# Squares of three blocks folded to 64 columns, rows of two blocks scaled on another engine, and an addition moved by a tile, in the first layer of a two-layer transformer kernel

## The chip, the cores and the metric

The kernel runs on one core of a Trainium2 chip. The metric is the device time of one execution in microseconds (us); the time given for a kernel is the median of its runs. A profile is one execution taken by the hardware profiler, with its own time. Engines are named as the profile names them: PE (TensorE, the matrix engine), PEld (its weight loads), DVE (VectorE), ACT (ScalarE), POOL (GpSimd) and SP (SyncE, which only issues transfers). Each takes its instructions in the order of the program and waits at an instruction whose inputs are not ready.

## The reference

Input x has 2048 tokens of 448 features. Two layers, with the same weights, each do

```python
x = x + A(layernorm(x), wqkv, wo)
x = x + B(layernorm(x), w_gate, w_up, w_down)

def A(x, wqkv, wo):
    q, k, v = heads(x @ wqkv)
    p = softmax(q @ k.T * 28 ** -0.5)
    return heads_back(p @ v) @ wo

def B(x, w_gate, w_up, w_down):
    return (sigmoid(x @ w_gate) * (x @ w_up)) @ w_down
```

with 16 heads of 28 features in A and 1792 hidden features in B.

## The kernel before, in words

**Blocks and tiles.** The 2048 tokens are four blocks of 512 (`TB` = 4 tiles of 128 tokens each). This text counts blocks and tiles from one; in the code block 1 is `b` = 0 and tile 1 is `i` = 0. The stages follow each other: projection of the first layer (about 12 to 120 us of the span), attention over 16 heads, output projection, the gated part, and the same for the second layer. The change lies in the projection of the first layer, function `project`.

**Queries and keys.** For each block `qk` (its loop begins at L865) makes 7 tiles of 128 features by 512 tokens. A tile is 11 matmuls (`by_features`, L649) into one of four PSUM banks in turn. ACT copies it to f16 (L883), DVE writes the rest that f16 loses (L884), ACT squares the copy (L886), and DVE folds the square by taking the larger of two halves (L890): once, from 512 to 256 columns. SP stores both f16 parts (L893). Three tiles later PE sums the folded squares of each head (`norm_products`, L845 and L848): one matmul of 256 columns for a tile, two for the fourth. At the end of a block DVE takes the largest of these sums (`finish`, L904). They bound the scores: `guard_of_norms`, in the first tile of the values of block 3, ends the sums of block 4, and the attention begins behind it.

**Values.** `vals` makes four tiles of 128 tokens by 448 features for each block (L671 to L676), which ACT copies out (L1136).

**Preparing a block.** Blocks 3 and 4 are normalised along the way. `norm` makes mean and variance of each of four row tiles on DVE (L340, L341) and the reciprocal deviation on POOL (L344, L346). `squares` scales each row tile on DVE (`scale`, L381) and turns it in squares of 32 on DVE (L398); `store` writes the result to DRAM and `gather` reads it back with features on the partitions, both on SP; `ready` splits it in f16 parts, ACT (L234, L239) and DVE (L235, L240) in turn. `norm_two` and `lift` (L366), used by the second layer, scale on ACT instead, with an offset that POOL works out (L355, L357).

**Measure** reads weight rows and adds up their squares on DVE (`add`, L1318 and L1322), six additions of 1.3 to 2.2 us.

**Order.** All orders are written out by hand. `along_values` and the lists `fill` tell what is issued behind which tile. Block 3: `norm` behind the third tile of the values of block 1, `squares` and `store` behind the fourth, `gather` behind the first tile of `qk` of block 2, `ready` behind its tiles 6 and 7. Block 4: `norm` behind tile 2 of `qk` of block 2, `squares` behind tiles 3 and 4, `store` behind tile 7, `gather` in the values of block 2, `ready` behind tiles 2 and 3 of `qk` of block 3. The six additions stand behind tiles 5, 6, 7 of block 3 and 1, 2, 3 of block 4.

Of the kernel before, what the change touches and what calls it, by code (L numbers as in the profile page):

```python
# [11 lines left out]
F32 = mybir.dt.float32  # L12
# [3 lines left out]
AF = mybir.ActivationFunctionType  # L16
ALU = mybir.AluOpType
AX = mybir.AxisListType

P = 128  # L20
# [7 lines left out]
TB = NT // NB  # L28
W = TB * P
# [48 lines left out]
ALONE = 3  # L78
CHUNK = D * NF // 7
SUMS_AT = ((("w", 3), 74), (("u", 0), 122), (("u", 6), 236))  # L80

N_SLOTS = 19
N_QUART = 12
# [44 lines left out]
def interleaved_layers(ctx: ExitStack, tc: tile.TileContext, x_in, wqkv, wo, w_gate, w_up,  # L128
                       w_down, out):
    nc = tc.nc  # L130
# [8 lines left out]
    uid = [0]  # L139
# [175 lines left out]
    class Block:  # L315
# [16 lines left out]
        def norm(self, js=range(TB)):  # L332
# [12 lines left out]
                                    op1=ALU.mult)  # L345
            nc.gpsimd.tensor_tensor(rs, rs, nhalf[:, c], op=ALU.pow)  # L346

        def norm_two(self, j):

            self.norm((j, j + 1))  # L350
            if j == 0:
                self.off = cpool.tile([P, TB], F32, name=f"off_{uid[0]}", tag="off", bufs=4)
                self.lifted = {}
            off = self.off[:, j:j + 2]
            nc.gpsimd.tensor_tensor(off, self.mv[:, j:j + 2, 0], self.rs[:, j:j + 2],  # L355
                                    op=ALU.mult)
            nc.gpsimd.tensor_scalar(off, off, -1.0, None, op0=ALU.mult)  # L357

        def lift(self, j):
            if self.apart:  # L360
# [30 lines left out]
        def squares(self, js=range(TB)):  # L391
            if js[0] == 0:
                self.xn = big.get("xn", [P, TB, D])
                self.xs = big.get("xs", [P, NQ, TB, 32])
            xn, xs = self.xn, self.xs
            for j in js:
                self.scale(j)
                nc.vector.transpose(xs[:, :, j, :], xn[:, j, :])  # L398
            if js[-1] < TB - 1:
                return  # L400
            big.put(xn)
# [419 lines left out]
    def project(layer, wq, begun):  # L821
# [12 lines left out]
        def qk(b, blk, fill, before, ahead=()):  # L834
            pn = [bank(4 + 2 * (b % 2), "qnorm"), bank(5 + 2 * (b % 2), "knorm")]
            late = deque()
            few = W // 2

            def rows_of_heads(i):

                return ind[:, i:i + P // H, :].rearrange("p a h -> p (a h)")

            def norm_products(i, sq):
                if i <= 3:
                    nc.tensor.matmul(pn[0][:, 0:few], rows_of_heads(i), sq[:, 0:few],  # L845
                                     start=(i == 0), stop=(i == 3))
                if i >= 3:
                    nc.tensor.matmul(pn[1][:, 0:few], rows_of_heads(1 + i), sq[:, 0:few],  # L848
                                     start=(i == 3), stop=(i == 6))
                qrt.put(sq)  # L850

            def products(pm, i, some=range(11)):
                c = slice(i * P, (i + 1) * P)
                by_features(pm, blk, lambda kt: wq.qk[0][:, kt, c],
                            lambda kt: wq.qk[1][:, kt, c], some)

            begun = deque()
            if layer == 0 and b == 0:
                begun.extend(bank(i, "qkp") for i in range(2))
                for i, some in ((0, (0, 3, 1, 6, 2, 5, 8, 4)), (1, (0, 3, 6)), (0, (7,)),  # L860
                                (1, (1, 4, 7)), (0, (9, 10))):
                    products(begun[i], i, some)
            rest = {0: (), 1: (2, 5, 8, 9, 10), 4: (0, 3, 6, 1, 4, 7, 9, 2, 5, 8, 10)}

            for i in range(7):  # L865
                c = slice(i * P, (i + 1) * P)
                pm = begun.popleft() if begun else bank(evac[0] % 4, "qkp")
                evac[0] += 1
                if layer == 0 and b == 0:
                    products(pm, i, rest.get(i, range(11)))  # L870
                else:
                    products(pm, i)
                if layer == 0 and b == 0:
                    along[i]()
                if before and i in (1, 2):
                    before(i == 2)
                if len(late) == 3:
                    late.popleft()()
                hl = qrt.get("qkhl", [P, 2, W], F16)
                sq = qrt.get("sq", [P, W], BF16)  # L880
                if i < len(ahead) and ahead[i]:
                    ahead[i]()
                nc.scalar.activation(hl[:, 0, :], pm, AF.Copy, scale=PS)  # L883
                nc.vector.scalar_tensor_tensor(hl[:, 1, :], pm, PS, hl[:, 0, :], op0=ALU.mult,  # L884
                                               op1=ALU.subtract)
                nc.scalar.activation(sq, hl[:, 0, :], AF.Square)  # L886

                for n in (W // 2, P):
                    if n >= few:
                        nc.vector.tensor_tensor(sq[:, 0:n], sq[:, 0:n], sq[:, n:2 * n],  # L890
                                                op=ALU.max)
                n = slice(b * W, (b + 1) * W)
                nc.sync.dma_start(qk_scr[c, :, n], hl)  # L893
                qrt.put(hl)
                late.append(lambda i=i, sq=sq: norm_products(i, sq))
                if i < len(fill) and fill[i]:
                    fill[i]()

            def finish(whole=True):

                while len(late) > (0 if whole else 1):
                    late.popleft()()
                for i in range(2 if whole else 0):
                    nc.vector.tensor_reduce(peaks[:, i, b:b + 1], pn[i][0:H, 0:few], axis=AX.X,  # L904
                                            op=ALU.max)
            return finish
# [260 lines left out]
        if layer == 0:  # L1167
            def scaled(*js):
                if js[0] == 0:
                    b1.xn = big.get("xn", [P, TB, D])  # L1170
                for j in js:
                    b1.scale(j)

            def turned(kts):
                b1.turn_banks(6, kts)
                for j in range(TB):
                    b1.turn(j)
                b1.turned_high()
                b1.turned_low()

            fill = [idle, idle, lambda: b1.norm([0, 1]), lambda: b1.norm([2, 3]),
                    lambda: scaled(0)]
            ahead = [idle] * 5 + [lambda: scaled(1, 2, 3)]
            tell = Measure()
            along_values = {0: lambda: (b1.parts(), turned([0, 1]), tell.read(2)),
                            1: lambda: (turned([2, 3]), big.put(b1.xn), tell.read(2)),
                            2: lambda: (fin(), b2.norm(), tell.read()),
                            3: lambda: (b2.squares(), b2.store(), tell.read())}
        if layer == 0:
            fin = qk(0, blks[0], fill, None, ahead)  # L1190
            vals(0, blks[0], along_values)
            fill = [b2.gather, b3.norm, sq(3, 0, 1), sq(3, 2, 3), idle,
                    lambda: b2.ready(0, 1), lambda: (b2.ready(2, 3), b3.store())]
            fin = qk(1, b1, fill, None)
            vals(1, b1, {0: b3.gather, 2: fin})
            add = tell.add
            fin = qk(2, b2, [idle, lambda: b3.ready(0, 1), lambda: b3.ready(2, 3), idle, add, add,
                             add], None)
            fin = qk(3, blks[3], [add, add, add], fin)
        else:  # L1200
            b2.clear()
            ones_of_values()
            b3.apart = True
            h2, h3, s3 = b2.half_steps(), b3.half_steps(), b3.squared()
            both = lambda *steps: lambda: [do() for do in steps]
            order = (3, 0, 1, 6)
            fin = qk_sums(0, blks[0], {0: b1.later + s3[0:1], 1: h2[0:1], 2: h2[1:2], 3: s3[1:2],
                                       4: h2[2:3], 5: [s3[2], s3[3], s3[6]]})
            vals(0, blks[0], {0: both(s3[4], s3[7]), 1: both(s3[5], s3[8], h2[3]),
                              2: both(fin, s3[9], b3.store, h2[4]),  # L1210
                              3: both(h2[5], b3.gather, b3.clear)}, banks=order)
            fin = qk_sums(1, b1, {0: h2[6:7], 1: h2[7:8], 3: h2[8:9], 4: h2[9:10]})
            vals(1, b1, {1: both(fin, h3[0]), 2: both(*h3[1:3]), 3: both(*h3[3:5])}, banks=order)
            fin = qk_sums(2, b2, {0: h3[5:6], 1: h3[6:7], 2: h3[7:8], 3: h3[8:9], 4: h3[9:10]},
                          None, True)
            fin = qk_sums(3, b3, {}, fin)
# [1101 lines left out]
```

## Time and profile before

| | us |
|---|---|
| median of 3 runs (1869.34 to 1869.78) | 1869.38 |
| the profiled execution, its own time | 1869.45 |
| its span, from the first to the last instruction | 1867.7 |
| PE busy in the span | 1861.4 |
| PEld busy | 1416.1 |
| DVE busy | 1462.4 |
| ACT busy | 1404.2 |
| POOL busy | 306.4 |

The table is read from the top: between the profiled execution's own time and its span lie 1.75 us of start and end, and its time stands 0.07 us above the median. PE is busy almost all the time, but the ends of its matmuls are modelled, so that its share says little by itself; what counts is how far apart its matmuls start, and who is late in each stage.

### The profile page before, as it was taken

To read this page: it belongs to the slowest core of one execution; us is meant where nothing else is said; L and a number is where in the kernel's file an instruction comes from. 1 tells how busy PE (TensorE), PEld (TensorE's weight loads), DVE (VectorE), ACT (ScalarE), POOL (GpSimd) and SP (SyncE) were. 2 spreads that over 40 slices of the span, in tenths; PEclk is the share of its full clock that TensorE was granted. 3 is DMA by queue.
4 is the path that set the end of the run, shared out by engine and by line. 5 is a ranking of instruction groups with operands and counts; after the bars stand their busy time and mean duration, and the time that the engine had idled before them with its cause. 6 is when DMAs were issued, how large, how long until landed. Compare 5 with 4: busy or idle time off the path is not lost. (4 is left out here: it accounts for less than half of the span.)

```text
span 1867.7 us, 57157 instructions
## 1 busy us (share of the span) xinstructions
PE 1861.4 (100%) x24479; PEld 1416.1 (76%) x24479; DVE 1462.4 (78%) x2933; ACT 1404.2 (75%) x1865; POOL 306.4 (16%) x582
## 2 busy tenths in 40 slices
PE   9999999999999999999999999999999999999999
PEld 4455566656565899999987568888877668999999
DVE  7748898998997888788877477777777688887764
ACT  6569999999993655555567899999999746555541
POOL 3001123453412111212122000000000031121110
PEclk9999999999999999999999999999999999999999
DMA  7674454454433866757764322122120258677653
GB/s 265 182 214 130 131 160 128 125 156 113 136 129 86 288 211 229 244 204 257 243 187 109 88 52 52 27 53 52 30 50 14 79 165 264 210 249 239 235 201 144
DMA packets 114885, 286.24 MB, mean 153 GB/s; under 512 B 15134, under 2 KB 68878, under 8 KB 114496
## 3 DMA queue, kind: packets, MB, share of 16 engines
q0 software_dynamic: 35088, 174.86, 27.8%
q1 hardware_dynamic: 78384, 106.27, 20.3%
q8 instruction: 194, 3.18, 0.7%
q10 hardware_dynamic: 1152, 1.38, 0.3%
q14 instruction: 67, 0.55, 0.1%
HBM read 218.20 MB, written 54.29 MB: 146 GB/s over the span
## 5 line engine op out<-in xcount | busy, mean ns | idle before, releaser
L1574 ACT ACTIVATE prob_s<-sc 128x1536 f32<-128x1536 f32 (+1 forms) x657 | 888.1, 1484 | 5.9 <-PE sc L1559 3.0
L1609 PE MATMUL acc<-prob_s,val_s 128*32 128x256 f32 (+3 forms) x7708 | 587.2, 384 | 0.0
L1559 PE MATMUL sc<-qp_s 114*32 114x512 f16 x7868 | 571.3, 379 | 0.0
L1559 PEld LDWEIGHTS <-qp_s 114*32 114x32 f16 x8192 | 309.9, 96 | 168.8 <-issue 70.8
L1609 PEld LDWEIGHTS acc<-prob_s,val_s 128*32 128x32 f32 x7708 | 314.1, 110 | 100.3 <-issue 9.2
L1944 PE MATMUL dnp<-dn_s,hparts_s 128*128 128x224 f16 x2184 | 245.8, 259 | 0.0
L664 PEld LDWEIGHTS <-gue_s 128*128 128x128 f16 x2240 | 218.8, 98 | 24.5 <-PE op L1738 0.7
L1944 PEld LDWEIGHTS <-hparts_s 128*128 128x128 f16 x2184 | 210.2, 98 | 5.1
L664 PEld LDWEIGHTS <-gul_s 128*128 128x128 f16 x2016 | 197.0, 98 | 19.9
L664 PE MATMUL chain<-xwide_s,gue_s 128*128 128x256 f16 x1680 | 210.9, 273 | 0.0
L1589 DVE SCALAR_TENSOR_TENSOR power_q<-power_q,expo_q 128x512 f32<-128x512 f32 x243 | 168.2, 692 | 8.3
L664 PE MATMUL side<-xshort_s,gul_s 128*128 128x256 f16 x1344 | 165.0, 273 | 0.0
L2017 ACT COPY one_q<-chain 128x256 f32<-128x256 f32 x224 | 83.1, 372 | 105.4 <-PE chain L664 104.6
L2033 DVE TENSOR_TENSOR one_q<-side,one_q 128x512 f32<-128x512 f32 x112 | 74.3, 689 | 39.1 <-PE side L664 38.8
L1638 DVE STREAM_TRANSPOSE oturned_q<-acc 128x512 f32<-128x512 f32 x32 | 23.0, 717 | 98.4 <-PE acc L1609 98.2
L2044 ACT ACTIVATE one_q<-one_q 128x512 f32<-128x512 f32 x56 | 35.3, 630 | 79.8 <-DVE one_q L2033 79.8
L1609 PE MATMUL acc<-power_q,val_s 128*32 128x256 f32 (+3 forms) x300 | 94.2, 396 | 0.0
L1584 DVE TENSOR_SCALAR expo_q<-aside,base 128x512 f32<-128x512 f32 x81 | 60.6, 748 | 40.5 <-PE aside L1559 40.1
L587 POOL TENSOR_SCALAR rs<-mv 128x1 f32<-128x1 f32 x8 | 1.5, 191 | 505.8 <-DVE mv L585 505.8
L664 PE MATMUL chain<-xshort_s,gul_s 128*128 128x256 f16 x672 | 82.5, 273 | 0.0
L1902 DVE TENSOR_TENSOR hparts_s<-hsums_q,hparts_s 128x256 f16<-128x256 f32 (+1 forms) x152 | 71.3, 519 | 11.1 <-ACT hparts_s L1898 11.1
L664 PE MATMUL side<-xwide_s,gue_s 128*128 128x256 f16 x560 | 79.4, 273 | 0.0
(273 smaller groups left out, 2559.0 us busy)
## 6 DMA issues: line engine op xcount, KB each, us to landing
gue_s<-gu_early POOLq DMA_DIRECT2D x52, 960.0 KB, 5.3
gul_s<-gu_late POOLq DMA_DIRECT2D x52, 768.0 KB, 4.7
dn_s<-dn_parts POOLq DMA_DIRECT2D x42, 784.0 KB, 6.7
qp_s<-qk_scr SPq DMA_DIRECT2D x96, 224.0 KB
xt_scr<-xs_s SPq DMA_DIRECT2D x48, 224.0 KB
xraw_s<-xt_scr SPq DMA_DIRECT2D x12, 768.0 KB
qk_scr<-qkhl_q SPq DMA_DIRECT2D x28, 256.0 KB
qp_s<-qk_scr SPq DMA_DIRECT2D x64, 112.0 KB
```

Source lines behind the costliest of these rows:

```text
L664: nc.tensor.matmul(pm, a, x, start=(first and i == 0), stop=(i == len(terms) - 1), skip_group_check=True)
L1559: nc.tensor.matmul(ps[32 * j:32 * j + 32, :], hd.k[:, keys], hd.q[:, qb * W:(qb + 1) * W], start=True, stop=True, tile_position=(0, 32 * j))
L1574: nc.scalar.activation(prob[:, 0:n, :], ps[:, 0:n, :], AF.Exp, scale=exp_scale)
L1584: nc.vector.tensor_scalar(y, ps, base2[:, 0:1], -116.0, op0=ALU.mult, op1=ALU.max)
L1589: nc.vector.scalar_tensor_tensor(p, p, c[k], y, op0=ALU.add, op1=ALU.mult)
L1609: nc.tensor.matmul(acc[qb * VC:(qb + 1) * VC, s], v[:, kc % TB, h, :], probs[c * NB + qb][:, s], start=(kc == 0 and a == 0), stop=(kc == N ...
L1638: nc.vector.transpose(turned.rearrange("p b c -> p (b c)"), acc)
L1902: nc.vector.tensor_tensor(to[:, :, 1], a, to[:, :, 0], op=ALU.subtract)
L1944: nc.tensor.matmul(pm, a[:, x, t], w[:, p, y], start=(begin and n == 0 and (j == 0 or alone)), stop=(n == 2), skip_group_check=True)
L2017: nc.scalar.copy(to, pm)
L2033: nc.vector.tensor_tensor(one[m], side[m], one[m], op=ALU.add)
L2044: nc.scalar.activation(out, v, AF.Sigmoid, scale=gate_scale)
```

## The change

The squares of blocks 2 to 4 of the first layer are folded three times, from 512 to 256, 128 and 64 columns, and the sums of heads and their maxima take 64 columns; block 1 stays at 256. The rows of blocks 3 and 4 are scaled by ACT, `squares` issuing all scalings of its call before its turns, with an offset that POOL works out behind the deviation. The additions stand behind tiles 4, 5, 6, 7 of block 3 and 1, 2 of block 4.

```diff
+FOLDED_FROM = 1
...
+        def offset(self, j, n):
+            if j == 0:
+                self.off = cpool.tile([P, TB], F32, name=f"off_{uid[0]}", tag="off", bufs=4)
+            off = self.off[:, j:j + n]
+            nc.gpsimd.tensor_tensor(off, self.mv[:, j:j + n, 0], self.rs[:, j:j + n],
+                                    op=ALU.mult)
+            nc.gpsimd.tensor_scalar(off, off, -1.0, None, op0=ALU.mult)
...
             for j in js:
-                self.scale(j)
+                nc.scalar.activation(xn[:, j, :], x[:, self.b * TB + j, :], AF.Identity,
+                                     scale=self.rs[:, j:j + 1], bias=self.off[:, j:j + 1])
+            for j in js:
                 nc.vector.transpose(xs[:, :, j, :], xn[:, j, :])
...
-            few = W // 2
+            few = 64 if b >= FOLDED_FROM else W // 2
...
-                for n in (W // 2, P):
+                for n in (W // 2, P, 64):
                     if n >= few:
                         nc.vector.tensor_tensor(sq[:, 0:n], sq[:, 0:n], sq[:, n:2 * n],
                                                 op=ALU.max)
...
-                            2: lambda: (fin(), b2.norm(), tell.read()),
+                            2: lambda: (fin(), b2.norm(), b2.offset(0, TB), tell.read()),
...
-            fill = [b2.gather, b3.norm, sq(3, 0, 1), sq(3, 2, 3), idle,
+            fill = [b2.gather, lambda: (b3.norm(), b3.offset(0, TB)), sq(3, 0, 1), sq(3, 2, 3), idle,
...
-            fin = qk(2, b2, [idle, lambda: b3.ready(0, 1), lambda: b3.ready(2, 3), idle, add, add,
+            fin = qk(2, b2, [idle, lambda: b3.ready(0, 1), lambda: b3.ready(2, 3), add, add, add,
                              add], None)
-            fin = qk(3, blks[3], [add, add, add], fin)
+            fin = qk(3, blks[3], [add, add], fin)
```

`norm_two` of the second layer calls `offset` in place of the same lines; what it issues stays as it was.

## Rows read from the trace of the kernel before

**Rows 1.** The page, part 1: busy us (share of the span) and instructions.

```profile
PE 1861.4 (100%) x24479; PEld 1416.1 (76%) x24479; DVE 1462.4 (78%) x2933; ACT 1404.2 (75%) x1865; POOL 306.4 (16%) x582
```

**Rows 2.** Timeline of PE, in the projection: start, us, instruction, count.

```profile
57.46 0.27 PE L845 MATMUL qnorm<-sq_q,ind 128*128 128x256 bf16 x1
...
93.43 2.54 PE L649 MATMUL qkp<-xhl_s,wqk_s 128*128 128x512 f16 x11
...
95.91 2.54 PE L649 MATMUL qkp<-xhl_s,wqk_s 128*128 128x512 f16 x11
...
103.07 0.49 PE L848 MATMUL knorm<-sq_q,ind 128*128 128x256 bf16 x3
```

**Rows 3.** Windows of 20 us: length, busy us (count) of PE, PEld, DVE, ACT, POOL, clock, DMA.

```profile
40.00:60.00 20.00, 20.00 (x99) 9.48 (x98) 17.43 (x41) 7.91 (x13) 4.19 (x7) 1.00 0.85 293
...
80.00:100.00 20.00, 20.00 (x99) 9.51 (x98) 19.76 (x41) 12.18 (x21) 0.00 (x0) 1.00 0.33 111
```

**Rows 4.** Timeline of DVE, 76 to 104 us; in brackets idle time before and its cause.

```profile
76.61 1.29 DVE L235 TENSOR_TENSOR xhl_s<-xraw_s,xhl_s 128x512 f16<-128x512 f32 x2 [3.75 <-ACT xhl_s L234]
...
98.98 0.28 DVE L890 TENSOR_TENSOR sq_q<-sq_q 128x256 bf16<-128x256 bf16 x1
99.18 0.69 DVE L884 SCALAR_TENSOR_TENSOR qkhl_q<-qkp,qkhl_q 128x512 f16<-128x512 f32 x1
99.78 0.29 DVE L890 TENSOR_TENSOR sq_q<-sq_q 128x256 bf16<-128x256 bf16 x1
101.60 0.69 DVE L884 SCALAR_TENSOR_TENSOR qkhl_q<-qkp,qkhl_q 128x512 f16<-128x512 f32 x1 [1.53 <-ACT qkhl_q L883]
```

**Rows 5.** Timeline of ACT, 40 to 78 us.

```profile
50.21 0.60 ACT L883 ACTIVATE qkhl_q<-qkp 128x512 f16<-128x512 f32 x1 [1.12 <-PE qkp L649]
50.84 0.63 ACT L886 ACTIVATE sq_q<-qkhl_q 128x512 bf16<-128x512 f16 x1
...
60.31 1.14 ACT L234 CAST xhl_s<-xraw_s 128x512 f16<-128x512 f32 x2 [3.87 <-DMA xraw_s<-xt_scr]
...
75.96 1.14 ACT L234 CAST xhl_s<-xraw_s 128x512 f16<-128x512 f32 x2 [3.42 <-DMA xraw_s<-xt_scr]
```

**Rows 6.** Groups of PE by line and shape: busy us, mean ns of one, idle us.

```profile
L845 PE MATMUL qnorm<-sq_q,ind 128*128 128x256 bf16 x16 | 4.4, 272 | 0.0
L923 PE MATMUL norms<-sq_q,ind 128*128 128x64 bf16 x64 | 3.3, 193 | 0.0
```

**Rows 7.** Groups of DVE by line and shape, columns as in rows 6.

```profile
L890 DVE TENSOR_TENSOR sq_q<-sq_q 128x256 bf16<-128x256 bf16 x28 | 7.9, 282 | 0.0
L961 DVE TENSOR_TENSOR sq_q<-sq_q 128x128 bf16<-128x128 bf16 x28 | 6.3, 225 | 1.0
...
L1101 DVE TENSOR_REDUCE peaks<-norms 16x1 f32<-16x128 f32 x8 | 1.9, 271 | 0.7 <-PE norms L923 0.7
...
L904 DVE TENSOR_REDUCE peaks<-qnorm 16x1 f32<-16x256 f32 x4 | 1.6, 407 | 0.1
```

**Rows 8.** Timeline of DVE in the second layer, where squares are folded twice.

```profile
957.24 0.54 DVE L961 TENSOR_TENSOR sq_q<-sq_q 128x256 bf16<-128x256 bf16 x2
957.70 0.69 DVE L488 TENSOR_TENSOR xwide_s<-t_q,xwide_s 128x512 f16<-128x512 f32 x1
```

**Rows 9.** Timeline of POOL, 40 to 60 us.

```profile
52.70 1.03 POOL L346 TENSOR_TENSOR rs<-rs,nhalf 128x4 f32<-128x4 f32 x1
```

**Rows 10.** Groups of POOL by line and shape, columns as in rows 6.

```profile
L357 POOL TENSOR_SCALAR off<-off 128x2 f32<-128x2 f32 x20 | 7.0, 352 | 1.8
...
L355 POOL TENSOR_TENSOR off<-mv,rs 128x2 f32<-128x2 f32 x20 | 5.1, 255 | 1.6
```

**Rows 11.** Timeline of ACT in the second layer, scalings back to back.

```profile
962.66 2.05 ACT L366 ACTIVATE lifts_s<-x,off,rs 128x448 f32<-128x448 f32 x3
964.62 0.52 ACT L1136 ACTIVATE val_s<-vp 128x448 f32<-128x448 f32 x1
```

**Rows 12.** Timeline of PE, first microseconds.

```profile
1.34 5.72 PE L313 MATMUL still<-still_q 128*128 128x512 f16 x13 [1.34 <-DVE warm L191]
```

More of the change, by code (lines that the diff above doesn't have):

```diff
@@ L351, in norm_two @@
             if j == 0:
-                self.off = cpool.tile([P, TB], F32, name=f"off_{uid[0]}", tag="off", bufs=4)
                 self.lifted = {}
[L354 to L357, printed above, removed]
+            self.offset(j, 2)
         def lift(self, j):
```

## The prediction, made before the changed kernel was run

> **What bounds the kernel now.** The page's first part gives PE 1861.4 busy us in a span of 1867.7 [rows 1]. As the ends of matmuls are modelled, that doesn't prove that PE sets the pace; its timeline does, in the stretch that is changed. There 11 matmuls of 512 columns and one product of 256 columns begin again every 95.91 - 93.43 = 2.48 us [rows 2]; the 2.54 us of the eleven overlap the next row, and no idle time stands beside them. So PE runs without a pause, and a shorter product is worth its columns, if everybody else keeps up. Who might not is read from the windows [rows 3]: at 80 to 100 us DVE is busy 19.76 of 20 us, PE 20.00, ACT 12.18. DVE's own timeline shows why [rows 4]: it stood idle 3.75 us, began the splitting of block 4's rows at 76.61, and from there worked off a queue (splits, tiles, six additions) without an idle row until the tile whose fold starts at 99.78. Only the next tile finds it waiting, 1.53 us, for ACT. PE doesn't feel this, since a fold is wanted three tiles later. The idle time before 76.61 comes from ACT, which waited 3.42 us for the transfer of block 4's rows and took them at 75.96 [rows 5]. So two engines are full at once, and DVE's slack is what it has left at the last tile.
>
> **The change, part by part.** I make the sum against the profiled execution's own time, 1869.45, which is 0.07 above the median.
>
> *PE's gain.* A product of 256 columns takes 272 ns, one of 64 columns in the second layer 193 [rows 6]; their difference of 79 ns, over 8 products in each of 3 blocks, is 24 x 0.079 = 1.9 us. It counts only where PE isn't made to wait.
>
> *DVE's cost.* A lone fold of 256 columns lasts 282 ns [rows 7], but the next instruction starts 0.20 us after it, at 99.18 after 98.98 [rows 4]; by that spacing the queue of before was free at 99.78 + 0.20 = 99.98. Where folds follow each other, each must wait for the one before. In the second layer two folds take 0.54 us, of which the last is 0.225, so the second starts 0.32 after the first, and the next instruction 0.46 after the first, 0.14 after the second [rows 7, 8]. A third has no row. It starts when the second has ended (0.225 + 0.035 = 0.26), and lets the next start after 0.12, an estimate from 0.20 and 0.14 for 256 and 128 columns. Three folds: 0.32 + 0.26 + 0.12 = 0.70, against 0.20: +0.50 us a tile. From below it is 0.26, if the third hides altogether (0.46 - 0.20); from above 0.61, if the last holds the engine for its whole 0.225. I take 0.50, since the chained rows show this very kind of instruction. [...]
>
> *What DVE gets back.* A maximum over 256 columns takes 407 ns, over 128 columns 271 [rows 7]; at 64 I take 0.20, so two maxima (block 3's) save 0.4 us in the queue. The eight scalings leave DVE, but all of them before its idle time at 76.61, so they help only if block 4's rows land earlier.
>
> *Do they land earlier?* Rather later. The deviation of block 4 is ready on POOL at 52.70 + 1.03 = 53.73 [rows 9]. Now two tiles with 0.50 more each stand before it on DVE (+1.0), and two offset instructions behind it on POOL, 0.26 and 0.35 in the second layer [rows 10], with their gaps 0.75: 55.5. There ACT waits, and behind it in ACT's queue stands the copy of tile 4, which before began at 50.21 [rows 5]. Two scalings take 0.65 each (three of them and the next instruction: 964.62 - 962.66 = 1.96) [rows 11]; tile 4 is copied at 56.8. Its copy, rest and three folds take 0.6 + 0.7 + 0.8, and PE wants the fold at 57.46 [rows 2], so a pause of some 1.5 us opens there. Then come three tiles of 1.2 (0.60 + 0.63), two more scalings, and ACT reaches block 3's rows at 56.8 + 3.6 + 1.3 = 61.7 instead of 60.31 [rows 5]; DVE, with folds of tiles 4 to 6 before it, is as late. The last tile, the store behind it on SP, and the gather follow by the same amount: block 4 starts on DVE at 76.61 + 1.4 = 78.0. Bounds: 76.2 (the queue as before, and block 3's store a little earlier, as DVE's turns no longer alternate with scalings), 79.2 (POOL at its slower, two short waits more). For block 3's own scalings ACT has room, 7.91 busy of 20 us [rows 3], and POOL's two weight transfers behind the offset leave 0.7 us later, 30 us before they are added up.
>
> *The additions.* Six additions stay in the same queue, one tile sooner: DVE has no idle time there, so nothing is won or lost at the end. The tiles behind them are late one tile sooner, PE's pauses with them.
>
> *The sum.* DVE's queue from 78.0: before's 99.98 - 76.61 = 23.37; 11 tiles (5 of block 3, 6 of block 4) x 0.50 = 5.5; maxima -0.4. The last tile can start at 106.5 and needs 0.60 (99.18 to 99.78) + 0.32 + 0.26 + 0.20 = 1.4: its fold is ready at 107.9. PE wanted it at 103.07 + 2 x 0.11 = 103.3 as the third of three products [rows 2], and 1.8 us earlier with the short products. So DVE sets the end, PE's gain is lost in its waits (some 6 us of them), and the projection ends 107.9 - 103.3 = 4.6 us later. All that follows (sums, bound, first scores) hangs on this product and moves as one. 1869.45 + 4.6 - 0.07 = 1873.98; I say **1873.9**, as a busier DVE waits less for ACT inside its queue.
>
> **The rivals.**
> 1. *Not slower: block 4's rows land early.* With four scalings off DVE for each block, DVE and SP could pass block 4 on sooner. The queue needs 23.37 + 5.5 - 0.4 + 1.4 = 29.9 us and PE wants the end at 101.5, so it decides from a start at 71.6, 5.0 us sooner than now. Then only PE's 1.9 counts: 1867.5. For it speaks DVE's idle 3.75 us; against it that ACT waited 3.87 us for block 3's rows at 60.31 [rows 5], a transfer that the change hardly moves, and everything of block 4 stands behind it. Chance 0.06.
> 2. *Short folds are cheap.* At the lower bound of 0.26 a tile the queue is 11 x 0.24 = 2.6 shorter, its start 0.7 and its last tile 0.2 sooner: 4.5 - 3.5 = +1.0, 1870.4. Against it: the 225 ns row. [...] Chance 0.13.
> 3. *The clock falls in PE's new pauses.* [...] At the start 13 matmuls of 512 columns took 5.72 us, 0.43 each, twice as long as later [rows 12]. Four tiles at that pace take 4.7 us each where DVE's pace allows about 3.5: +5, 1878.7. Chance 0.05.
>
> **How the numbers follow.** My forecast has 0.76, and its own range is 1872.4 to 1875.5: the start of DVE's queue by -1.0 or +1.1, the fold by -0.05 or +0.11 a tile. The predicted time is its middle, 1873.9. For 8 in 10 I go down to rival 2 without its lower half, 1870.6, and up to 1876.2; out stay rival 1, the rest of 2, rival 3. A measurement of this kernel can tell 0.2% (3.7 us) from no change: above 1873.1 is slower. Of the forecast some 0.57 lies above it, with rival 3 0.62; below 1865.6 no case goes, as PE's gain is 1.9: 0.02; the rest, 0.36, is the same.
>
> **What would show it.** Right: waits of PE for DVE's folds at L845 and L848, about 1.6 us at tile 4 of block 2 and some 1 us each at the last tiles of block 3 and the first of block 4; ACT waiting for POOL's offset at about 54; three folds of one tile 0.70 from the first to the next instruction; DVE without idle time from 78 to 107; clock 1.00 throughout. Wrong: if the split of block 4's rows begins before 76, if the three folds take under 0.5, or if PE shows no wait in block 4.

## The result, and the profile after

The changed kernel takes **1875.12 us** (median of 8 runs, 1874.83 to 1875.48), the kernel before 1869.52 in the same series: a ratio of 1.0029, interval 1.0021 to 1.0038. It is slower by 5.6 us, 0.3%. The prediction was 1873.9, in a range from 1870.6 to 1876.2. The profiled execution of the changed kernel took 1875.44, with a span of 1873.7; so it stands 5.99 above that of before.

The first view is the timeline of PE in the projection of the changed kernel: start, us, instruction, count, idle time before it and what ended it.

```profile
12.08 1.19 PE L657 MATMUL qkp<-xhl_s,wqk_s 128*128 128x512 f16 x4 [0.50 <-DVE wqk_s L247]
...
55.05 2.54 PE L657 MATMUL qkp<-xhl_s,wqk_s 128*128 128x512 f16 x11
59.01 0.20 PE L853 MATMUL qnorm<-sq_q,ind 128*128 128x64 bf16 x1 [1.43 <-DVE sq_q L898]
...
79.45 2.54 PE L657 MATMUL qkp<-xhl_s,wqk_s 128*128 128x512 f16 x11
81.83 0.19 PE L853 MATMUL qnorm<-sq_q,ind 128*128 128x64 bf16 x1
81.86 2.54 PE L657 MATMUL qkp<-xhl_s,wqk_s 128*128 128x512 f16 x11
...
90.33 0.20 PE L856 MATMUL knorm<-sq_q,ind 128*128 128x64 bf16 x1 [1.10 <-DVE sq_q L898]
...
93.83 0.20 PE L856 MATMUL knorm<-sq_q,ind 128*128 128x64 bf16 x1 [0.92 <-DVE sq_q L898]
...
97.32 0.20 PE L853 MATMUL qnorm<-sq_q,ind 128*128 128x64 bf16 x1 [0.92 <-DVE sq_q L898]
...
102.67 0.20 PE L853 MATMUL qnorm<-sq_q,ind 128*128 128x64 bf16 x1 [0.22 <-DVE sq_q L898]
...
107.80 0.20 PE L856 MATMUL knorm<-sq_q,ind 128*128 128x64 bf16 x1 [0.36 <-DVE sq_q L898]
```

Where PE isn't kept waiting, a tile now begins every 81.86 - 79.45 = 2.41 us instead of 2.48 [rows 2]: the product of 64 columns is worth its 0.07 to 0.08. But six times PE stands before a product until DVE's last fold is there. The brackets add up to 5.0 us, but they start at the modelled end of the matmul before. Counted by starts it is more: the tile that begins at 55.05 would take 2.38 (81.83 - 79.45) up to its product, which starts at 59.01, so PE loses 1.58 there, not 1.43. By starts there are seven waits (1.58, 1.26, 1.08, 1.08, 0.14, 0.38, 0.52), together 6.05 us.

The last product of block 4, the third of the row at 103.07 in [rows 2] (103.28), starts at 107.80. I call it *the last product*; it is 4.52 later. Not all of this is the change: the first matmul of the projection, which no edit touches, starts at 12.08 here and in the kernel before at

```profile
11.88 1.19 PE L649 MATMUL qkp<-xhl_s,wqk_s 128*128 128x512 f16 x4 [0.50 <-DVE wqk_s L245]
```

Such a difference arises from one execution to the next (the table below shows it for every kernel). Counted from that matmul the last product is 4.31 later (differences are taken before rounding), and this is what the change costs in the projection. It fits the waits: 6.05 less 4.31 is 1.74, what PE won by the 23 shorter products ahead of the last (23 x 0.079 = 1.8).

The cause of the waits is on DVE. Its timeline, in the stretch that answers to [rows 4]:

```profile
78.24 1.29 DVE L237 TENSOR_TENSOR xhl_s<-xraw_s,xhl_s 128x512 f16<-128x512 f32 x2 [3.70 <-ACT xhl_s L236]
...
98.44 0.69 DVE L892 SCALAR_TENSOR_TENSOR qkhl_q<-qkp,qkhl_q 128x512 f16<-128x512 f32 x1
99.05 0.77 DVE L898 TENSOR_TENSOR sq_q<-sq_q 128x256 bf16<-128x256 bf16 x3
99.74 1.15 DVE L1326 CUSTOM_DVE_ANT_0 junk_s<-raw_s,sums 128x896 bf16<-128x896 f32 x1
...
106.38 0.68 DVE L892 SCALAR_TENSOR_TENSOR qkhl_q<-qkp,qkhl_q 128x512 f16<-128x512 f32 x1
106.98 0.77 DVE L898 TENSOR_TENSOR sq_q<-sq_q 128x256 bf16<-128x256 bf16 x3
107.66 0.15 DVE L308 SCALAR_TENSOR_TENSOR back<-pw 128x1 f32<-128x1 f32 x1
```

The queue starts at 78.24 instead of 76.61 (1.42 later, counted from the first matmul), no row up to the last fold has idle time in brackets, and from the first of three folds to the next instruction pass 99.74 - 99.05 = 0.69 us, where one fold took 0.20. The groups of DVE by shape, 40 to 110 us (busy us, mean ns of one, idle us before them), which answer to [rows 7]:

```profile
L898 DVE TENSOR_TENSOR sq_q<-sq_q 128x256 bf16<-128x256 bf16 x21 | 5.9, 283 | 0.0
L898 DVE TENSOR_TENSOR sq_q<-sq_q 128x128 bf16<-128x128 bf16 x21 | 4.7, 225 | 0.7
L898 DVE TENSOR_TENSOR sq_q<-sq_q 128x64 bf16<-128x64 bf16 x21 | 4.0, 192 | 0.7
L912 DVE TENSOR_REDUCE peaks<-qnorm 16x1 f32<-16x64 f32 x3 | 0.6, 205 | 0.0
```

Each chained fold also leaves 0.7 / 21 = 0.03 us idle while it waits for the one before.

Why the queue starts later is seen on ACT and POOL. ACT, answering to [rows 5]:

```profile
55.59 1.41 ACT L403 ACTIVATE xn_s<-x,off,rs 128x448 f32<-128x448 f32 x2 [4.78 <-POOL off L356]
56.91 0.57 ACT L891 ACTIVATE qkhl_q<-qkp 128x512 f16<-128x512 f32 x1
...
61.64 1.12 ACT L236 CAST xhl_s<-xraw_s 128x512 f16<-128x512 f32 x2
...
77.59 1.14 ACT L236 CAST xhl_s<-xraw_s 128x512 f16<-128x512 f32 x2 [3.86 <-DMA xraw_s<-xt_scr]
```

POOL, answering to [rows 9]:

```profile
53.92 1.04 POOL L348 TENSOR_TENSOR rs<-rs,nhalf 128x4 f32<-128x4 f32 x1
55.04 0.20 POOL L354 TENSOR_TENSOR off<-mv,rs 128x4 f32<-128x4 f32 x1
55.33 0.23 POOL L356 TENSOR_SCALAR off<-off 128x4 f32<-128x4 f32 x1
```

The deviation comes 1.2 later than before, the offset ends at 55.56, ACT's first scaling waits for it, and the copy of tile 4 behind the scaling starts at 56.91 instead of 50.21. That makes PE's first pause, and ACT takes block 3's rows at 61.64 instead of 60.31. Tile 7 of block 2 is then late as well, and on SP the store of block 4's rows stands behind its store. SP's rows, first before, then changed:

```profile
63.44 3.49 SPq L410 DMA_DIRECT2D xt_scr<-xs_s  x4
...
65.25 3.49 SPq L418 DMA_DIRECT2D xt_scr<-xs_s  x4
```

From this store to ACT's copy of block 4's rows pass 12.5 us before (75.96 in [rows 5]) and 12.3 us here (77.59): the rows land later because they leave later.

The clock stayed up in these pauses. The windows of the changed kernel, columns as in [rows 3]:

```profile
40.00:60.00 20.00, 18.57 (x92) 8.45 (x91) 14.80 (x38) 10.83 (x19) 5.07 (x11) 1.00 0.88 302
80.00:100.00 20.00, 17.07 (x85) 7.29 (x83) 19.28 (x46) 11.41 (x21) 0.00 (x0) 1.00 0.24 79
```

So of the 5.99 us between the two profiled executions 0.21 arise before the change is reached, 4.31 in the projection, and 1.47 behind it, where the prediction put nothing; e14 and e15 below turn to that part.

### The profile page after: what moved, and what is told of

Same layout as the page of the kernel before. It is cut to its first block, busy times and chain, and to the rows that moved or that the text cites. A ratio compares the mean times of both kernels' runs of the same rounds, so it can differ in the third digit from the quotient of the medians.

```text
span 1873.7 us, 57202 instructions
## 1 busy us (share of the span) xinstructions
PE 1862.2 (99%) x24479; PEld 1355.9 (72%) x24479; DVE 1465.9 (78%) x2967; ACT 1409.0 (75%) x1873; POOL 308.5 (16%) x586
## 5 line engine op out<-in xcount | busy, mean ns | idle before, releaser
L1617 PE MATMUL acc<-prob_s,val_s 128*32 128x256 f32 (+3 forms) x7708 | 574.2, 383 | 0.0
L1567 PE MATMUL sc<-qp_s 114*32 114x512 f16 x7868 | 557.0, 379 | 0.0
L1567 PEld LDWEIGHTS <-qp_s 114*32 114x32 f16 x8192 | 281.9, 96 | 195.2 <-issue 84.5
L1617 PEld LDWEIGHTS acc<-prob_s,val_s 128*32 128x32 f32 x7708 | 282.6, 110 | 132.8 <-issue 11.1
```

The lines of the kernel that those rows point to most:

```text
L1567: nc.tensor.matmul(ps[32 * j:32 * j + 32, :], hd.k[:, keys], hd.q[:, qb * W:(qb + 1) * W], start=True, stop=True, tile_position=(0, 32 * j))
L1617: nc.tensor.matmul(acc[qb * VC:(qb + 1) * VC, s], v[:, kc % TB, h, :], probs[c * NB + qb][:, s], start=(kc == 0 and a == 0), stop=(kc == N ...
```

## The experiments

**The theory, Q:** DVE's queue, from the split of block 4's rows to the last fold, sets the end; three chained folds cost it 0.49 us a tile, and it starts 1.4 later. **Rivals:** S, ACT's wait for POOL's offset makes the loss; A, the moved additions make it. For every profiled execution the table gives, against before: the start of the projection's first matmul (11.88 before); the last product, counted from that matmul; what arises behind the last product; the time (1869.45 before), which is the sum of these three; and, not as a difference, ACT's idle time in the attention of both layers: all gaps over 0.05 us between its first and its last score activation, but for one of 0.33 near the start that every kernel has in each layer.

| kernel | median | start | last product | behind it | time | ACT idle |
|---|---|---|---|---|---|---|
| changed | 1875.12 | +0.21 | +4.31 | +1.47 | +5.99 | 1.12 |
| e1_folds_only | 1874.09 | +0.06 | +4.93 | -0.22 | +4.76 | 0.00 |
| e2_scaling_only | 1869.75 | -0.01 | +0.22 | +0.29 | +0.49 | 0.06 |
| e3_additions_back | 1874.07 | -0.26 | +4.95 | -0.07 | +4.62 | 0.06 |
| e5_additions_only | 1870.12 | -0.14 | -0.01 | +0.94 | +0.79 | 0.83 |
| e4_two_folds | 1872.39 | -0.08 | +1.79 | +1.58 | +3.29 | 1.12 |
| e13_rows_later | 1872.35 | -0.08 | +3.11 | -0.16 | +2.87 | 0.00 |
| e6_additions_early | 1869.14 | -0.07 | -0.11 | +0.08 | -0.11 | 0.00 |
| e7_early_rows_later | 1868.88 | -0.17 | -1.22 | +0.92 | -0.48 | 0.61 |
| e10_early_two_folds | 1869.49 | -0.13 | -1.23 | +1.19 | -0.17 | 0.63 |
| e14_after_old_buffers | 1875.01 | -0.13 | +4.29 | +1.40 | +5.56 | 1.13 |
| e15_before_new_buffers | 1869.43 | +1.10 | -0.01 | +0.09 | +1.18 | 0.00 |

e14 and e15 issue in the projection just what the changed kernel and the kernel before issue, and their last products come within 0.02 of these. The medians belong to four series, in which the kernel before took 1869.46 (e1, e2, e3, e5), 1869.53 (e4, e6, e7, e10), 1869.82 (e13, e14, e15) and 1869.52 (the changed kernel). Starts that are compared between executions below are counted from the first matmul ("from equal starts").

**One part at a time: e1, e2, e3, e5.** e1 is the kernel before with

```diff
-            few = W // 2
+            few = 64 if b >= 1 else W // 2
-                for n in (W // 2, P):
+                for n in (W // 2, P, 64):
```

> The kernel before with the three folds alone: DVE scales block 4's rows as before, the additions stand where they stood. Theory Q (DVE's queue between the split of block 4's rows and the last fold sets the end; three chained folds cost it 0.49 us a tile): the two folded tiles ahead of the scalings make them 1.0 later and three more tiles delay the rows further, so the split begins some 1.7 later than 76.6, at about 78.3; 11 tiles x 0.49 = 5.4, maxima -0.4, the last fold +0.5 to its end: PE's last norm product some 4.3 later than 103.3, and the time 1873.8, or up to 1875 if the smaller rest that the changed kernel shows behind the projection comes with it. Rival S (it is the wait of ACT for POOL's offset that makes the loss): without it PE's 1.9 us should be won, 1867.6, or at most be eaten up, 1869.5. Rival A (the additions, one tile sooner, make PE wait): they are back, so 1869.5 or less.

e2 is the changed kernel with `FOLDED_FROM = 4` (no block is folded further) and the additions at their old places.

> The scaling on ACT with POOL's offset alone; squares folded to 256 columns and additions where before has them. Theory Q: the fold of tile 4 of block 2 comes late because its copy stands behind the scalings on ACT (PE waits up to 0.4 there, since that tile needs one fold instead of three), the split of block 4's rows begins within 0.6 of before's 76.6, and the end is +0.4: 1869.5 to 1870.2. Rival S: most of the 5.6 us, 1873 to 1875. Rival A: 1869.5.

e3 is the changed kernel with the lists

```diff
-            fin = qk(2, b2, [idle, lambda: b3.ready(0, 1), lambda: b3.ready(2, 3), add, add, add,
+            fin = qk(2, b2, [idle, lambda: b3.ready(0, 1), lambda: b3.ready(2, 3), idle, add, add,
                              add], None)
-            fin = qk(3, blks[3], [add, add], fin)
+            fin = qk(3, blks[3], [add, add, add], fin)
```

> The changed kernel with the six additions back at their old tiles. Theory Q: the same work stands in the same full queue, so the end doesn't move, 1874.8 to 1875.4; only PE's waits for folds move a tile later, out of tiles 6 and 7 of block 3 into block 4. Rival A: near 1869.5 to 1871. For the part of the difference that arises behind the projection (about 1 us, in the attention stages): if it comes from the order in which the additions' scratch tiles take their buffers, it goes here, 1874.0; if not, it stays.

and e5 the kernel before with the opposite edit.

> The kernel before with the six additions one tile sooner and nothing else. Theory Q: nothing moves at the end, 1869.5, at most one short wait of PE at tile 7 of block 3. Rival A: a good part of the 5.6 us, over 1871. If the order of the scratch buffers costs the attention stages something, 1870 to 1870.5.

Measured: e1 1874.09 (ratio 1.0024, 1.0015 to 1.0033), e2 1869.75 (1.0003, 0.9994 to 1.0012), e3 1874.07 (1.0024, 1.0015 to 1.0034), e5 1870.12 (1.0004, 0.9995 to 1.0013). The folds alone make the whole loss in the projection, the scaling alone 0.22, the additions alone none: S and A fall. e1's last product, +4.93, is later than the 4.3 expected, and the timeline of DVE in e1 shows a part of why:

```profile
78.70 1.29 DVE L235 TENSOR_TENSOR xhl_s<-xraw_s,xhl_s 128x512 f16<-128x512 f32 x2 [3.81 <-ACT xhl_s L234]
```

Without ACT's help the rows come even later, at 78.70 and not 78.3, since the scalings stand behind folds on DVE: the store of block 4's rows starts 0.5 later than in e3, from equal starts. The later start is 0.34 of the 0.6 beyond the 4.3; the rest lies in the expectation, as the prediction's own sum from a start at 78.3 gives +4.9. e1 and e3 differ only in how the rows are scaled, and end level, +4.93 and +4.95: e3's queue starts 0.33 sooner but is 0.36 longer, so no gain of the scaling on ACT is seen at the end.

e3 has PE's waits one tile later, as expected, but doesn't end where the changed kernel ends: its last product is 0.64 later. 0.28 of this is the start of the queue (78.31 against 78.03, from equal starts), though the store of block 4's rows starts alike in both (65.02 and 65.04), so it arose on the rows' way and not by the edit. The other 0.36 is the longer queue, and a row of DVE in e3, behind the second addition, shows most of it:

```profile
90.37 0.69 DVE L892 SCALAR_TENSOR_TENSOR qkhl_q<-qkp,qkhl_q 128x512 f16<-128x512 f32 x1 [0.29 <-ACT sq_q L894]
```

In the changed kernel, with the additions a tile sooner, DVE has no such gap. e3's time is yet 1.05 below the changed kernel's, because what arises behind the projection is gone. e5 gains that part in its profiled execution and nothing else; its interval includes no change.

**Two folds: e4.** The changed kernel with

```diff
-            few = 64 if b >= FOLDED_FROM else W // 2
+            few = P if b >= FOLDED_FROM else W // 2
```

> The changed kernel with two folds instead of three (squares to 128 columns, products and maxima of 128). Theory Q: a tile costs DVE's queue 0.46 - 0.20 = 0.26 more than before instead of 0.49, 11 tiles x 0.26 = 2.8; the split of block 4's rows begins about 0.7 sooner than in the changed kernel, maxima -0.3; PE's last norm product comes 1.0 to 1.3 later than before's 103.3, and with 0 to 1 us that the attention stages add the time is 1870.5 to 1871.8. If the third fold were hidden behind the second, as the cheap-folds rival has it, the time would stay within 0.5 of the changed kernel's 1875.1. If the loss came from ACT's wait for POOL's offset, which is untouched, it would stay too.

Measured: 1872.39 (1.0015, 1.0006 to 1.0025). The third fold isn't hidden: without it the last product comes 4.31 - 1.79 = 2.52 sooner. Its cost stands in DVE's timeline of e4:

```profile
96.95 0.54 DVE L898 TENSOR_TENSOR sq_q<-sq_q 128x256 bf16<-128x256 bf16 x2
97.41 1.15 DVE L1326 CUSTOM_DVE_ANT_0 junk_s<-raw_s,sums 128x896 bf16<-128x896 f32 x1
```

Two folds hold the queue 0.46, the third adds 0.69 - 0.46 = 0.23, over 11 tiles 2.5; the queue starts 0.46 sooner (from equal starts). The sum, 3.0 less 0.1 for longer maxima, is more than the 2.52 found, and the +1.79 is above the 1.0 to 1.3 that I expected. The timeline of PE in e4 shows what is missing from the sum: in the last product's row

```profile
104.88 0.33 PE L856 MATMUL knorm<-sq_q,ind 128*128 128x128 bf16 x3
```

PE waits for nothing. DVE had caught up by then; PE had lost its time further up, 0.9 before 58.11 (tile 4 of block 2) and 0.26, 0.83 and 0.83 before 88.68, 91.95 and 95.22, where the additions stand in the queue, and can't win it back: by starts its waits are 2.98 us, less 1.2 for 23 products that are 0.053 shorter. When the queue is nearly short enough, its worst point is among the additions, not at the last tile.

**The queue's start: e13.** The changed kernel, with block 4's `squares` behind tiles 4 and 5:

```diff
-            fill = [b2.gather, lambda: (b3.norm(), b3.offset(0, TB)), sq(3, 0, 1), sq(3, 2, 3), idle,
+            fill = [b2.gather, lambda: (b3.norm(), b3.offset(0, TB)), idle, sq(3, 0, 1), sq(3, 2, 3),
```

> The changed kernel with block 4's scalings and turns one tile later (tiles 4 and 5 of block 2), so that the copy of tile 4 no longer stands behind ACT's wait for POOL's offset; the additions where the change has them. It tells the two parts of theory Q apart: the later landing of block 4's rows against the folds in the queue behind it. The pause of 1.8 at tile 4 of block 2 should shrink to under 0.5 and the split of block 4's rows begin 1.2 to 1.3 sooner than in the changed kernel, at about 77; the queue behind it is as long, so PE's last norm product moves by just that: +2.8 to +3.3 against before, the time 1873.4 to 1874.0. If the start of the queue doesn't count, it stays at 1875.1.

Measured: 1872.35 (1.0015, 1.0005 to 1.0024). The timeline of DVE in e13:

```profile
76.75 1.29 DVE L237 TENSOR_TENSOR xhl_s<-xraw_s,xhl_s 128x512 f16<-128x512 f32 x2 [3.65 <-ACT xhl_s L236]
```

From equal starts the queue begins 1.20 sooner (76.83 against 78.03), and the last product comes 4.31 - 3.11 = 1.20 sooner: one for one, as a full queue does, and as expected. The pause at tile 4 of block 2 is gone; one of 0.48, by starts, stands before the last products of that block instead. The time is below the expected 1873.4, because what arises behind the projection is gone too.

**The queue emptied: e6, e7, e10.** If DVE's full stretch is the cause, work taken out of it must give back all. e6 is the changed kernel with four additions moved into DVE's idle time ahead of 78 us:

```diff
-            vals(1, b1, {0: b3.gather, 2: fin})
             add = tell.add
+            vals(1, b1, {0: b3.gather, 2: fin, 3: lambda: (add(), add())})
-            fin = qk(2, b2, [idle, lambda: b3.ready(0, 1), lambda: b3.ready(2, 3), add, add, add,
-                             add], None)
-            fin = qk(3, blks[3], [add, add], fin)
+            fin = qk(2, b2, [add, lambda: (add(), b3.ready(0, 1)), lambda: b3.ready(2, 3), idle, idle,
+                             add, add], None)
+            fin = qk(3, blks[3], [], fin)
```

> The changed kernel with four of the six additions taken out of DVE's full stretch into its idle times before the split of block 4's rows (two behind the last tile of block 2's values, one each at tiles 1 and 2 of block 3), two at tiles 6 and 7 of block 3, none in block 4. Folds and scaling untouched. Theory Q: four additions of 0.86 to 1.2 leave the queue between 78 and the last fold, so the last fold is ready some 4 us sooner, at about 103.4 against 107.8: PE waits only at tile 4 of block 2 (1.7, for the fold behind ACT's late copy), which eats its gain of 1.9, and the end is within 0.3 of before's; with 0 to 1 us from the attention stages 1869.2 to 1870.5. If not DVE's queue but the later landing of block 4's rows sets the end, nothing moves: 1874 to 1875.

e7 has e13's edit as well.

> As the run with the additions early, and block 4's scalings and turns one tile later (tiles 4 and 5 of block 2 instead of 3 and 4), so that the copy of tile 4 isn't behind ACT's wait for POOL's offset. Theory Q: the pause of 1.7 at tile 4 of block 2 shrinks to 0.4 at most and PE keeps most of its 1.9: its last norm product 1.4 to 1.5 sooner than before's 103.3, the time 1867.9 to 1868.9 with 0 to 1 us from the attention stages. If the pauses of PE cost nothing at the end, it equals the run with the additions early.

e10 is e7 with two folds.

> As the run before this one, with two folds instead of three. Theory Q: PE gains less by a product (0.053 instead of 0.079, by 24: 1.3), and nothing makes it wait: -1.3, 1868.1 to 1869.1 with 0 to 1 us from the attention stages. If three folds still cost something in the run before, this one is the faster of the two.

Measured: e6 1869.14 (0.9998, 0.9989 to 1.0007), e7 1868.88 (0.9997, 0.9988 to 1.0006), e10 1869.49 (1.0000, 0.9991 to 1.0009). The timeline of DVE in e6 has a late start too, but slack behind it:

```profile
78.49 1.29 DVE L237 TENSOR_TENSOR xhl_s<-xraw_s,xhl_s 128x512 f16<-128x512 f32 x2 [0.50 <-ACT xhl_s L236]
...
99.20 0.69 DVE L892 SCALAR_TENSOR_TENSOR qkhl_q<-qkp,qkhl_q 128x512 f16<-128x512 f32 x1 [0.96 <-ACT qkhl_q L891]
```

From equal starts the split begins half a microsecond later than in the changed kernel, as ACT takes block 4's rows only when DVE is through with the fourth moved addition, by what the profile gives as the end of its wait:

```profile
77.84 1.14 ACT L236 CAST xhl_s<-xraw_s 128x512 f16<-128x512 f32 x2 [4.42 <-DVE part L1326]
```

All 21 tiles are folded three times, and still the last product comes 4.42 sooner: the theory's sharpest test. The four additions are longer than expected, 2.0 to 2.2 us each from start to next start in the changed kernel (83.46 to 85.43 for the first), not 0.86 to 1.2; so 8.6 us leave the queue, more than the loss, and DVE now waits for ACT. PE's only wait of size is that at tile 4 of block 2 (1.56 by starts), and it eats the gain. In e7 that wait is gone too, and PE's gain is there, 1.22 of the 1.8 that the 23 shorter products ahead of the last are worth; two waits, 0.48 and 0.13 by starts, hold the rest. Of e7's 1.22 little is left in the time, since 0.92 arises behind the projection; against before it is no difference that can be measured. It has the lowest median of all versions, 6.2 us below the changed kernel's. e10 is level with e7 in the projection (-1.23): it has no wait, but its products are worth only 23 x 0.053 = 1.2, so what the third fold gives PE in e7 goes into e7's two waits.

**What arises behind the projection: e14, e15.** It is either about 0 (-0.22 to 0.29, seven kernels with before) or 0.92 to 1.58 (six), with nothing between, and idle time of ACT in the attention goes with it, though it is smaller (0.6 to 1.1). By the first and last score activations of each layer, 0.91 of the changed kernel's 1.47 arise in the first layer's attention and 0.63 in the second's. The timeline of ACT in the second layer's attention of the changed kernel:

```profile
1224.42 4.14 ACT L1582 ACTIVATE prob_s<-sc 128x1536 f32<-128x1536 f32 x3 [0.21 <-PE aside L1567]
...
1311.86 1.46 ACT L1582 ACTIVATE prob_s<-sc 128x1536 f32<-128x1536 f32 x1 [0.26 <-ACT prob_s L1582]
...
1399.31 2.79 ACT L1582 ACTIVATE prob_s<-sc 128x1536 f32<-128x1536 f32 x2 [0.26 <-ACT prob_s L1582]
```

Every 87.4 us ACT, else without a gap, stands still for about a quarter of a microsecond. In e3 the same stretch has no such row. These gaps are a sign of the loss and not its measure: e5 has four of them there, 0.39 us together, and its second attention is 0.13 shorter than before's. The windows, first of the changed kernel (length, then PE, PEld, DVE, ACT, POOL):

```profile
1250.00:1370.00 120.00, 120.00 (x2192) 82.81 (x2188) 89.13 (x145) 119.74 (x89) 0.00 (x0) 1.00 0.21 50
```

and of e3:

```profile
1250.00:1370.00 120.00, 120.00 (x2198) 77.28 (x2193) 88.88 (x144) 120.00 (x89) 0.00 (x0) 1.00 0.22 49
```

(PEld's figures differ too, but don't tell the two kinds apart: in this window the kernels without gaps have 77 to 106, those with gaps 75 to 85.)

After e1 to e5 it looked as if the moved additions did this: they change the order in which the 12 small buffers come free, and so where the attention's small tiles lie. e14 puts that order back in the changed kernel, with no instruction touched, and e15 puts the changed kernel's order into the kernel before:

```diff
             fin()
+            if layer == 0:
+                qrt.free = deque([7, 6, 2, 8, 5, 10, 11, 3, 0, 4, 1, 9])
             heads[0].load()
```

> The changed kernel, instruction for instruction; only the list of the 12 small buffers is put, between the projection and the attention, into the order that the kernel before has there (the moved additions had rotated it), so the attention's small tiles lie at before's addresses. For the about 1.2 us that this kernel, unlike those with the additions at their old tiles, adds in the attention stages. Theory B (addresses): that part goes, 1873.9 to 1874.3, and ACT has no idle time in the attention. Theory T (the phase between PE and ACT in which the attention happens to start): nothing changes, 1874.9 to 1875.4. The projection's 4.5 stays in either.

> The kernel before, instruction for instruction, with the small buffers put into the order of the changed kernel ahead of the attention. Theory B: the attention grows by 0.6 to 1.2 as in the run with the additions alone, 1870.1 to 1870.7, and ACT shows pauses of about 0.1 some 87 us apart. Theory T: 1869.5.

Measured: e14 1875.01 (1.0029, 1.0017 to 1.0040), e15 1869.43 (0.9999, 0.9990 to 1.0008). (e15's profiled execution lost 1.10 ahead of its first projection matmul, at a granted clock of 0.91 in its first 20 us; its median is near before's.) The order of these buffers isn't it. Nor is it the moved additions by themselves: e13 has them where the changed kernel has them, and shows none of it. What decides is open; a phase between PE and ACT in which the attention begins would fit, but no run sets that phase.

## Why the prediction was right, and where it fell short

From the starts of the changed kernel 0.21 us are taken off here, which its profiled execution lost ahead of the projection; the prediction's figures stand beside them.

- **PE's gain**, 0.079 a product: right. Unhindered tiles begin 2.41 apart instead of 2.48, the waits less the delay leave 1.74 for it in all, and e7 and e10 show the gain at the last product.
- **Three folds in 0.70 instead of 0.20:** right, 0.69. The third fold, which had no row, lasts 192 ns (the second 225), starts 0.26 after the second and lets the next start after 0.11 to 0.12. Rival 2, cheap short folds, falls by the 0.69 of the rows and by e4.
- **Block 4's rows land later:** right, 78.03 against 78.0, and rival 1 falls. The chain came as worked out: POOL's offset at 55.35 (55.5), the copy of tile 4 at 56.70 (56.8), block 3's rows on ACT at 61.43 (61.7). e13 shows that the late start counts one for one. What the prediction left open, e1 adds: with the folds there, scaling on DVE sends the rows off later still.
- **The pauses of PE:** right in place and, by starts, in size; 1.58 at tile 4 of block 2 (some 1.5), 1.26, 1.08 and 1.08 at the last tiles of block 3 and the first of block 4 (some 1), 6.05 in all (some 6).
- **The queue sets the end:** right. The last product was put at 107.9 and starts at 107.59; +4.31 against a sum of +4.6. From the split to the last tile the queue takes 28.1 us (78.24 to 106.38), where the sum has 28.5. e6, which empties the queue and leaves the rest, shows it from the other side.
- **The additions change nothing at the end:** right without the folds (e5: -0.01). Beside them it isn't quite so: DVE, which was said to have no idle time there, has 0.29 us of it in e3, and the move a tile sooner made the queue 0.36 shorter.
- **The clock** held at 1.00 through pauses of up to 1.43 us: rival 3 didn't come. That a fallen clock has the pace of the first 13 matmuls, as the rival reckons, no run shows.
- **What failed** is the sentence that all behind the last product "moves as one". 1.47 us of the profiled execution's 5.99 arise behind it, by the medians about 1.3 of 5.6 (5.6 - 4.3). Without them the kernel would take some 1869.52 + 4.31 = 1873.8, next to the 1873.9 predicted. The sum had this term at zero; the profile of before shows no gap on ACT there, and the prediction gives no other reason. What makes it stays open. That 1875.12 still lies in the range is luck in part: the range was built from the start of the queue and the price of the folds, which both came near their middle, and left no room for this term.

## What to carry to other kernels

When one engine gives work to another to save itself time, price the chain on the receiving engine at its spacing, not at its columns: three dependent folds that halve each time last 0.28, 0.23 and 0.19 us, little less each time, and hold the engine 0.69 us where one held it 0.20. Then ask where that engine is without idle time, and move what isn't urgent out of that stretch: here four additions, put where DVE stood idle, gave back all 4.3 us in the projection. Before two executions are compared, look where their difference begins: here up to 1.1 us arose before the changed stretch. A change of this kernel under 0.1% can't be credited to its cause, since the attention adds 0 or 0.9 to 1.6 us for reasons that the edit doesn't name.

## What the runs showed of the hardware that was not expected

- The attention has two paces. Thirteen kernels with the same instructions there show either no gap on ACT over 0.06 us or, in the second layer, gaps of 0.1 to 0.3 us some 87 us apart, and in the first a few more; with the gaps go 0.9 to 1.6 us in all. It repeats: all 8 runs of the changed kernel lie between 1874.83 and 1875.48, and 9 of e3's 10 below 1874.5 (1873.64 to 1874.65 in all). The addresses of the small buffers don't decide it (e14, e15).
- In e15's profiled execution the first matmul of the projection starts at 12.97, 1.10 later than before's, and no edit touches what lies ahead of it. Its window there, columns as in [rows 3]:

```profile
0.00:20.00 20.00, 16.20 (x68) 8.20 (x69) 12.58 (x33) 10.88 (x19) 9.71 (x32) 0.91 0.89 302
```

  The granted clock is 0.91 there and 1.00 from 20 us on. In narrower windows the profile gives 1.00 from 6 to 8 us, 0.52 from 8 to 10, 0.63 from 10 to 12 and 1.00 again from 12 on; PE had stood idle 1.89 us ahead of 7.83. In the kernel before PE stood idle 0.88 us there, and the clock shows 1.00 in the same windows. A single execution can thus differ by a microsecond before the change is reached.
- The way of block 4's rows out and back takes a different time from one execution to the next. From SP's store to ACT's copy pass 12.52 us before, 12.27 in e5 and 12.25 in e15, which issue the same up to there, and 12.34 in the changed kernel against 12.64 in e3. A start of the queue that differs by 0.3 between two single executions proves nothing about an edit.
